# Scoring two head pairs of granule 1 ahead of their granule, with half of its queries loaded first

## The chip, the cores and the metric

The kernel runs on one core of a Trainium2 chip. The metric is the device time of one execution in microseconds (us). The engines are named as in the profile: PE (TensorE matmuls, with PEld for its weight loads), DVE (VectorE), ACT (ScalarE), POOL (GpSimd) and SP (SyncE, which here issues every DMA). The kernel before takes 595.39 us, the median of 3 runs (595.28 to 595.61).

## The reference, cut to what matters

Three layers follow one another: a windowed attention, a gated layer of 512 x 2048 x 512 with Mish, and a bilinear layer of 512 x 1536 x 512.

```python
# q, k, v: (2, 8, 768, 64)      block = 32, window = 16
k_sum = k.reshape(B, H, nb, block, D).max(axis=3)
v_sum = v.reshape(B, H, nb, block, D).mean(axis=3)
scores_l = where(|i - j| < window, scale * q @ k.T, -1e9)
scores_s = scale * einsum('bhsd,bhnd->bhsn', q, k_sum) + log(block)
a = softmax(concat([scores_l, scores_s]))          # + 1e-9 in the denominator
x = (a @ concat([v, v_sum])).transpose(0, 2, 1, 3).reshape(B * S, H * D)
h = x @ w_in;  x = (h * tanh(softplus(h))) @ w_out # Mish
return (x @ w_a) * (x @ w_b) @ w_out2
```

## The kernel before

**Attention.** The 1536 tokens form six granules of 256 tokens (g = 0 to 5; 0 to 2 are the first batch). The eight heads are four pairs p = 0 to 3; a pair fills the 128 partitions with two heads of 64. For one granule and some pairs `batch_s` (L549) multiplies queries by the 96 keys of a window and by the 24 block maxima (PE lines L567 and L571, 16 records each for a pair). `weights` (L579) then turns the scores of one pair into softmax weights: four mask-and-minimum operations on DVE (L588), four exponentials on ACT (L594), and on DVE an addition (L597), a reciprocal (L599) and the scaling (L601). `batch_o` (L606) transposes the weights (L626), copies them out of PSUM (L377 on ACT or L378 on DVE), multiplies them by the window's values (L638) and splits the result into a rounded part XH (L377 or L378) and a rest XL (L668). The weights lie in a ring of four slots, `sa_o`. Granule 0 is scored pair by pair, all others two pairs at a time.

Granule 0 doesn't wait for the block means of the values. These means are made by `prep_v` (matmuls L492), copied by `keep_v` (L503) and multiplied in at the end (L651). For later granules one DMA per granule, `spread_v` (L507, shown as `attn<-attn`), lays the means under the value windows.

**The layers behind.** A weight chunk comes raw (512 KB) into one of three stage slots and is converted by `convert` and `split`: L688 or L691 on ACT, L693 and L696 (and a further one, L700, in the unsigned form) on DVE, a rounding on ACT (L377) and a difference on DVE (L708). L688 uses the table of the exponential; the unsigned form needs no table. The first layer's chunks 0 and 1 are multiplied by granule 0 (L897 into h, Mish L927, L944 into y), then by granule 1, and so on (`visits1`, L759). The later lines, L1076, L1121 and L1229, are the rest of the two layers and fill the time from about 130 us.

**Order.** A planner (`Plan.emit`, L89) orders all instructions of an engine when the kernel is built: each operation has a key, lowered so that its users can meet theirs, and a modelled clock picks the ready operation with the lowest key on each engine. The constants at L43 to L50 are that model. A change of ACT's table adds `TABLE_PENALTY` to a key, and on PE another kind of matmul adds `SHAPE_PENALTY`. Keys below -50 are pinned; they order the first DMAs. The opening's pinned keys stand at L761, L836, L840 and L849; `bt` and `out_t` (L807 to L815) are the keys of scoring and of the output of each granule and pair. Where PE has nothing ready early on, the planner puts in idle matmuls (L434) until `fill_end` (L441). The engines then run in that order and wait on semaphores.

The first DMAs of the kernel before are, in order: keys and queries of granule 0 for the pairs 0 to 3 (384 KB and 128 KB each), the value windows of granule 0 (224, 384 and 384 KB), chunk `in` 1 of the weights, the other values of the batch (four of 256 KB), chunk `in` 0, the queries of granule 1 (512 KB), its value windows (two of 512 KB) and chunk `out` 0.

Of the kernel before, what the change touches and what calls it, by code (L numbers as in the profile page):

```python
# [34 lines left out]
class Plan:  # L35
# [8 lines left out]
    SAME, PE_SHAPE = 0.02, 0.095  # L44
    SHAPE_PENALTY = 1.6
    PINNED = -50.0
    DMA_LEAD, DMA_TAIL, DMA_RAMP = 0.62, 2.18, 8.0
    BACKLOG, DMA_SLACK, DMA_RING = 4.0, 0.5, 8
    TABLE, TABLE_PENALTY = 1.3, 5.37
    WARM, PAGE, PE_LEAD, FETCH, FETCH_BUSY = 0.34, 256, 64, (6.4, 2.6), 46.0  # L50
# [38 lines left out]
    def emit(self):  # L89
# [7 lines left out]
        key = [0.0] * n  # L97
# [10 lines left out]
        ready = {e: [] for e in engines}  # L108
        free_at = {e: 0.0 for e in engines}
        bank_free, where, held = {b: 0.0 for b in range(8)}, {}, set()  # L110
# [12 lines left out]
        while done < n:  # L123
            best = None
            for e in engines:
                t = free_at[e]
# [91 lines left out]
            if delay:  # L218
                dma_free = max(dma_free, end + self.DMA_LEAD) + delay * (1.35 if 2.0 < dma_free < self.DMA_RAMP else 1.0)
                end = dma_free + self.DMA_TAIL  # L220
                landed.append(end)
# [19 lines left out]
def attention_mish_moe_bilinear_moe(  # L241
# [90 lines left out]
    q_o = [take(NP * GT) for _ in range(NQ)]  # L332
    sa_o = [take(GU * SW) for _ in range(NSA)]
    at_o = [take(GU * P) for _ in range(NAT)]
# [7 lines left out]
    ksum_o = [take(NB) for _ in range(NP)]  # L342
    st_o = [[take(GU) for _ in range(3)] for _ in range(NSA)]
    n_ext = max(top[0] - EXT, N_EXT)
# [95 lines left out]
    pe(-1.0, 0.22 * 8, warm_up, words=16, r=["warm"], w=["warmbank"], alloc=("warmbank",), free=["warmbank"])  # L440
    pl.fill, pl.fill_end = fill, T0 + -7.99  # L441

# [97 lines left out]
    def load_q(key, g):  # L540
        b, gi = divmod(g, NG)
        o = q_o[g % NQ]

        for p0, p1 in [(p, p + 1) for p in range(NP)] if g == 0 else [(0, NP)]:
            dma(key + 1.0 * p0, ar(o, NP, GT)[:, p0:p1, :],
                qT[b, p0:p1, :, gi * GT:(gi + 1) * GT].rearrange("n d t -> d n t"),
                w=[sb(o + p0 * GT, (p1 - p0) * GT)], nbytes=(p1 - p0) * P * GT * 4)

    def batch_s(key, g, ps):  # L549

        b, gi = divmod(g, NG)
        names = [("S", g, ps, h) for h in range(2)]
        half = [slice(h * U, (h + 1) * U) for h in range(2)]
        slots = [nxt("sa", sa_o) for p in ps]
        sks = [sb(so, GU * SW) for _, so in slots]

        def mm(env):
            bk = [bank[env[name]] for name in names]
            for k, p in enumerate(ps):
                qt, kt, ks = ar(q_o[g % NQ], NP, GT)[:, p, :], ar(kt_o[p], SK), ar(ksum_o[p], NB)  # L560
                for j in range(2):
                    c = (2 * k + j) * SW

                    for h, e in ((0, 0), (1, 1), (0, 1), (1, 0)):
                        u = 2 * j + e
                        k0 = U * (GU * gi + u)
                        nc.tensor.matmul(bk[h][half[e], c:c + WK], qt[half[h], u * U:(u + 1) * U],  # L567
                                         kt[half[h], k0:k0 + WK], start=True, stop=True)
                    for h, e in ((0, 0), (1, 1), (0, 1), (1, 0)):
                        u = 2 * j + e  # L570
                        nc.tensor.matmul(bk[h][half[e], c + WK:c + SW], qt[half[h], u * U:(u + 1) * U],  # L571
                                         ks[half[h], :], start=True, stop=True)

        rd = [x for p in ps for x in (sb(q_o[g % NQ] + p * GT, GT), sb(kt_o[p], SK), ("kpad", p), sb(ksum_o[p], NB))]
        pe(key, 0.58 * len(ps), mm, words=64 * len(ps), duty=0.69, table="quarters", r=rd, w=names + sks, alloc=tuple(names))
        for k, p in enumerate(ps):
            weights(key + 0.01 * k, g, p, names, k, *slots[k], ring["sa"] - len(ps) + k, k == len(ps) - 1)

# [27 lines left out]
    def batch_o(key, g, ps):  # L606
# [7 lines left out]
        for p in ps:  # L614
            so, born = st.pop(("a", g, p))
            alive("sa", sa_o, born)
            s = ar(so, GU, SW)
# [142 lines left out]
    size = lambda b: GT * len(gran2[b])  # L760
    w_dma = {("in", 0): -88.93, ("out", 0): -85.34, ("in", 1): -93.01}  # L761
    pace = (6.36, 5.0, 6.2, 6.0, 5.4)
    att_in = {0: 4, 1: 8, 2: 8}
# [40 lines left out]

    SIGN = (T0 + 32.36, tl + 20.0)

    batches = [(g, p) for g in range(B * NG) for p in range(NP)]  # L807
    bt, out_t = {}, {}
    BG, SP = (26.14, 40, 48, 59.27, 73.73), (0.5, 1.0, 1.0, 1.08, 1.43)
    for g, p in batches:  # L810
        if g == 0:
            bt[g, p] = 5.46 + 1.76 * p
        else:
            bt[g, p] = BG[g - 1] + SP[g - 1] * p
        out_t[g, p] = bt[g, p] + (7.82 if g else 11.69)  # L815

    eps = 1.0e-3
    first_use = {}
    for vi, b, c, ts, dt in steps1:
        for kind, d in (("in", 0.0), ("out", 1.22 * dt)):  # L820
            first_use.setdefault((kind, c), ts + d)
# [10 lines left out]
    for b in range(B):  # L832
        g0 = NG * b
        if b == 0:
            pieces = [(T_S[0], 2), (T_S[2], 2)]
            kv, kd, ev = 9.86, -92.86, 1.5  # L836
        else:
            pieces = [(T_S[0], 2), (Y1, 2)]
            kv, kd = bt[g0, 0] - 3.2, bt[g0, 0] - 13.1
            ev = end_o(g0 - 2) + eps  # L840
        at_time(ev, lambda kv=kv, kd=kd, b=b, x=pieces: prep_v(kv, kd, b, x))
        at_time(ev, lambda kv=kv, b=b: keep_v(kv + 0.5, b))
        for p in range(NP):
            kk, kd = (bt[g0, p] - 4.19, -100.0 + p) if b == 0 else (bt[g0, p] - 3.0, bt[g0, 0] - 6.96 + 0.5 * p)
            ev = end_s(g0 - 1) if b else 1.0
            at_time(ev, lambda kd=kd, b=b, p=p: load_k(kd, b, p))
            at_time(ev, lambda kk=kk, p=p: prep_k(kk, p))
    for g in range(B * NG):
        kq, kw = [(-99.5, -94.0), (-85.86, -85.4)][g] if g < 2 else (bt[g, 0] - 0.92, bt[g, 0] - 4.68)  # L849
        at_time(end_s(g - 2) if g >= 2 else 1.0, lambda k=kq, g=g: load_q(k, g))  # L850
        at_time(end_o(g - 2) if g >= 2 else 1.4, lambda k=kw, g=g: load_windows(k, g))
        if g:
            at_time(end_o(g - 2) + 3 * eps if g >= 2 else 1.6, lambda k=bt[g, 0], g=g: spread_v(k, g))
    for g in range(B * NG):
        for ps in ([(p,) for p in range(NP)] if g == 0 else [(0, 1), (2, 3)]):
            at_time(bt[g, ps[0]], lambda g=g, ps=ps: batch_s(bt[g, ps[0]], g, ps))
            at_time(out_t[g, ps[0]], lambda g=g, ps=ps: batch_o(out_t[g, ps[0]], g, ps))
# [9 lines left out]
    def need(kind, c):  # L867
        if (kind, c) not in w_at:
            load_w(first_use[kind, c] - 7.48, kind, c, slot_of[kind, c])

# [34 lines left out]
    def step1(i, vi, b, c, ts, dt):  # L905
# [19 lines left out]
        gh, gl = ar(ho, n), ar(go, n)  # L925
        ka = ts + 0.3 * dt
        act(ka, n, lambda env: nc.scalar.activation(out=g, in_=hp(env), func=AF.Mish),  # L927
# [5 lines left out]
        need("out", c)  # L933
        ky = ts + 2.26 * dt
        for m in range(KC):
# [322 lines left out]

    combine_x1(A_, t - 18.9)
    combine_x1(B_, t - 1.27)  # L1260
    done_l = set()
# [81 lines left out]
```

## Time and profile before

| | |
|---|---|
| median of 3 runs | 595.39 us |
| the profiled execution | 595.54 us |
| its span in the trace | 593.8 us |
| PE busy | 586.6 us (99%) |
| PE weight loads busy | 530.9 us (89%) |
| DVE busy | 489.2 us (82%) |
| ACT busy | 318.8 us (54%) |
| DMA moved | 54.89 MB |

The span runs from the first to the last instruction on the core; 1.74 us of the execution's time lie outside it. Times of rows count from the span's start. A busy share is an average over stages that differ, and a PE that is busy can be busy with idle matmuls, or at half clock. Shares of single stretches and the granted clock are therefore read from stretches of some microseconds.

### The profile page before, as it was taken

The numbers are of one execution on the slowest core, as the hardware profiler recorded it, in microseconds if no ns is written. First come the engines' busy times: TensorE is split into PE (matmuls) and PEld (weight loads), VectorE is DVE, ScalarE is ACT, GpSimd is POOL, SyncE is SP. The second block draws the span as 40 slices with busy tenths as digits, with TensorE's granted clock in tenths as the row PEclk, the third lists the DMA queues.
The fourth block names the chain that finished last, engine by engine and source line by source line (L and its number), as shares of the span: only waits on it lengthen the run. The fifth ranks groups of instructions, "written<-read, shape, count | busy, mean of one in ns | idle before, by whom it ended". The sixth has DMA issues, their size and how long they took to land.

```text
span 593.8 us, 10770 instructions
## 1 busy us (share of the span) xinstructions
PE 586.6 (99%) x4162; PEld 530.9 (89%) x4163; DVE 489.2 (82%) x1134; ACT 318.8 (54%) x711; POOL 6.7 (1%) x34
## 2 busy tenths in 40 slices
PE   9999999999999999999999999999999999999998
PEld 5788788889898899989999999999898999999896
DVE  6899999999999988979799998858686876855443
ACT  5699999457555555455376655444262434433030
POOL 3000000000000000000000000000000000000000
PEclk9899999999999999999999999999999999999999
DMA  9997700222233221222003133230122212300202
GB/s 282 348 345 221 224 20 3 71 72 72 71 107 106 73 71 72 72 71 72 0 1 100 43 107 111 103 107 20 52 72 71 108 35 72 107 0 2 89 18 107
DMA packets 22288, 54.89 MB, mean 92 GB/s; under 512 B 1917, under 2 KB 8061, under 8 KB 22237
## 3 DMA queue, kind: packets, MB, share of 16 engines
q1 hardware_dynamic: 22236, 54.21, 27.8%
q8 instruction: 32, 0.52, 0.4%
q14 instruction: 20, 0.16, 0.1%
HBM read 50.07 MB, written 3.15 MB: 90 GB/s over the span
## 4 chain that ended last, share of the span: by engine, by line
PE 92%; ACT 3%; DVE 3%; DMA 1%; issue 1%; ACTq 0%
PE bank L1076 44%; PE bank L1121 17%; PE bank L1229 17%; PE bank L944 5%; PE bank L897 4%; ACT attn L594 2%; PE bank L567 1%; PE bank L638 1%; DMA attn<-attn 1%; PE bank L626 1%; PE bank L434 1%; DVE attn L588 1%; ACT L927 1%; ACT rounded L377 0%; PE bank L571 0%
## 5 line engine op out<-in xcount | busy, mean ns | idle before, releaser
L1076 PE MATMUL bank<-rounded,wext 128*128 128x384 f32 x1176 | 213.8, 335 | 0.0
L1076 PEld LDWEIGHTS bank<-rounded,wext 128*128 128x128 f32 x1176 | 205.7, 188 | 3.5
L377 ACT CAST rounded<-arena 128x384 fp32r<-128x384 f32 (+2 forms) x145 | 80.8, 568 | 88.9 <-PE bank L1229 37.4
L1121 PE MATMUL bank<-rounded,wext 128*128 128x512 f32 (+1 forms) x456 | 104.7, 380 | 0.0
L1229 PE MATMUL bank<-wext,rounded 128*128 128x512 f32 (+2 forms) x441 | 100.0, 386 | 0.0
L1089 DVE TENSOR_TENSOR arena<-arena,bank 128x384 f32<-128x384 f32 x132 | 71.8, 550 | 31.2 <-PE bank L1076 23.1
L1229 PEld LDWEIGHTS bank<-wext,rounded 128*128 128x128 f32 x441 | 82.0, 188 | 16.3
L1121 PEld LDWEIGHTS bank<-rounded,wext 128*128 128x128 f32 x456 | 83.9, 188 | 12.6
L1085 ACT COPY arena<-bank 128x384 f32<-128x384 f32 x108 | 51.5, 478 | 56.5 <-PE bank L1076 53.8
L377 ACT CAST wext<-arena 128x512 fp32r<-128x512 f32 (+1 forms) x80 | 49.0, 621 | 33.2 <-PE bank L1076 12.7
L1076 PE MATMUL bank<-rounded 128*128 128x384 f32 x336 | 61.1, 335 | 0.0
L1076 PEld LDWEIGHTS bank<-rounded 128*128 128x128 f32 x336 | 58.5, 188 | 0.2
L1125 DVE TENSOR_TENSOR arena<-bank,arena 128x512 f32<-128x512 f32 (+1 forms) x76 | 49.9, 658 | 10.0 <-PE bank L1121 9.9
L1248 DVE TENSOR_TENSOR arena<-bank,arena 128x512 f32<-128x512 f32 (+2 forms) x37 | 25.0, 677 | 34.5 <-PE bank L1229 34.5
L708 DVE TENSOR_TENSOR wext<-arena,wext 128x512 fp32r<-128x512 f32 (+1 forms) x80 | 49.8, 639 | 0.7 <-ACT wext L377 0.3
L696 DVE SCALAR_TENSOR_TENSOR arena<-arena 128x512 uint32<-128x512 uint32 x68 | 46.6, 689 | 2.3 <-ACT arena L688 0.4
L708 DVE TENSOR_TENSOR rounded<-arena,rounded 128x384 fp32r<-128x384 f32 (+2 forms) x72 | 40.9, 583 | 4.8 <-ACT rounded L377 4.3
L594 ACT ACTIVATE attn<-attn 128x120 f32<-128x120 f32 x96 | 36.7, 386 | 7.6 <-DVE attn L588 7.5
L944 PE MATMUL bank<-rounded 128*128 128x512 f32 (+1 forms) x168 | 37.1, 367 | 0.0
L688 ACT ACTIVATE arena<-arena 128x512 f32<-128x512 f32 x38 | 25.8, 680 | 17.7 <-DMA arena<-in_w_out_dram 9.4
L897 PE MATMUL bank<-rounded 128*128 128x512 f32 (+1 forms) x168 | 35.3, 363 | 0.0
L897 PEld LDWEIGHTS bank<-rounded 128*128 128x128 f32 x168 | 28.1, 189 | 4.7
(75 smaller groups left out, 546.3 us busy)
## 6 DMA issues: line engine op xcount, KB each, us to landing
arena<-in_w_out_dram SPq DMA_DIRECT2D x28, 512.0 KB, 3.3
arena<-in_w_in_dram SPq DMA_DIRECT2D x16, 512.0 KB, 3.9
arena<-in_w_a_dram SPq DMA_DIRECT2D x12, 512.0 KB, 4.1
arena<-in_w_b_dram SPq DMA_DIRECT2D x12, 512.0 KB, 3.3
arena<-in_kT_dram SPq DMA_DIRECT2D x8, 384.0 KB, 9.6
out_dram<-arena SPq DMA_DIRECT2D x11, 256.0 KB, 2.0
attn<-in_qT_dram SPq DMA_DIRECT2D x5, 512.0 KB, 8.7
attn<-in_v_dram SPq DMA_DIRECT2D x3, 768.0 KB, 7.3
```

The source lines that it names most:

```text
L377: alts = [("ACT", act_us(n), lambda env: nc.scalar.copy(out=dst(env), in_=src(env))), ("DVE", dve2_us(n) if fast else dve_us(n), lambda en ...
L594: act(key, SW + 90, lambda env, x=x: nc.scalar.activation(out=s[:, x, :], in_=s[:, x, :], func=AF.Exp, scale=-1.0, bias=negm[:, x:x + 1], ...
L696: dve(key, 512, lambda env: nc.vector.scalar_tensor_tensor(out=f.bitcast(U32), in0=hw.bitcast(U32), scalar=3, in1=f.bitcast(U32), op0=ALU. ...
L708: dve(key, n, lambda env: nc.vector.tensor_sub(out=r32(lo[0]()), in0=src, in1=hi[0]()), r=rd + hi[1], w=lo[1])
L897: nc.tensor.matmul(like(dst, b), lt, rt, start=(j == 0), stop=(j == 3 * KC - 1))
L944: nc.tensor.matmul(yp, lt, r32(rt), start=(fst and j == 0), stop=(lst and j == 2))
L1076: nc.tensor.matmul(dst, lt, r32(rt), start=(start and i == 0 and j == 0), stop=(last and i == 1 and j == 2), skip_group_check=True)
L1085: act(k, TN, lambda env: nc.scalar.copy(out=dst[0], in_=bank[env[nm[z]]][:, 0:TN]), w=[nm[z]] + dst[1])
L1089: dve(k, TN, lambda env: op(out=dst[0], in0=dst[0], in1=bank[env[nm[z]]][:, 0:TN]), w=dst[1] + [nm[z]], free=[nm[z]] if free else [])
L1121: nc.tensor.matmul(dst, lt, rt, start=(q == 0), stop=(q == 5))
L1125: dve(k + 1.2, n, lambda env: nc.vector.tensor_add(acc, bank[env[yn]][:, 0:n].rearrange(*shape[2], **shape[3]), acc), w=[yn] + ak, free=[yn])
L1229: nc.tensor.matmul(dst, lt, rt, start=(opens and j == 0), stop=(closes and j == n_mm - 1))
```

## The change

Granule 1's queries come in two DMAs of 256 KB. The first one, for the pairs 0 and 1, has the key -97.2, between the queries of pair 2 and the keys of pair 3 of granule 0; the second keeps a place behind the value windows. The pairs 0 and 1 of granule 1 are scored singly (keys 8.0 and 20.0), and their weights lie in two further slots that use the memory of `T_S[2]`. Their output has the key 15.97 + 7.59. The values of the first batch come in two DMAs of 512 KB into `Y0`, ahead of both `in` chunks, and their means are one block of matmuls and no longer two. The pinned keys, several planner constants and many keys of the rest are set anew. The diff, cut to its core:

```diff
-    SHAPE_PENALTY = 1.6
+    SHAPE_PENALTY = 1.69
-    DMA_LEAD, DMA_TAIL, DMA_RAMP = 0.62, 2.18, 8.0
+    DMA_LEAD, DMA_TAIL, DMA_RAMP = 0.62, 1.62, 8.0
+    START, RAMP = 0.8, ((2.8, 1.0), (7.3, 1.75), (11.0, 1.0), (1.0e9, 0.95))
-    TABLE, TABLE_PENALTY = 1.3, 5.37
+    TABLE, TABLE_PENALTY = 1.3, 11.05
...
-    sa_o = [take(GU * SW) for _ in range(NSA)]
+    sa_o = [take(GU * SW) for _ in range(NSA)] + [T_S[2], T_S[2] + GU * SW]
...
-    pl.fill, pl.fill_end = fill, T0 + -7.99
+    pl.fill, pl.fill_end = fill, T0 + -11.04
...
-        for p0, p1 in [(p, p + 1) for p in range(NP)] if g == 0 else [(0, NP)]:
-            dma(key + 1.0 * p0, ar(o, NP, GT)[:, p0:p1, :],
+        for p0, p1 in [(p, p + 1) for p in range(NP)] if g == 0 else ([(0, 2), (2, NP)] if g == 1 else [(0, NP)]):
+            dma(-97.2 if g == 1 and p0 == 0 else key + 1.0 * p0, ar(o, NP, GT)[:, p0:p1, :],
...
-        slots = [nxt("sa", sa_o) for p in ps]
+        first = g == 1 and ps[0] < 2
+        slots = [(NSA + p, sa_o[NSA + p]) if first else nxt("sa", sa_o[:NSA]) for p in ps]
...
-    w_dma = {("in", 0): -88.93, ("out", 0): -85.34, ("in", 1): -93.01}
-    pace = (6.36, 5.0, 6.2, 6.0, 5.4)
+    w_dma = {("in", 0): -89.93, ("out", 0): -86.62, ("in", 1): -91.35}
+    pace = (6.36, 4.44, 6.2, 6.0, 5.4)
...
-    SIGN = (T0 + 32.36, tl + 20.0)
+    SIGN = (T0 + 28.01, tl + 20.0)
...
-    BG, SP = (26.14, 40, 48, 59.27, 73.73), (0.5, 1.0, 1.0, 1.08, 1.43)
+    BG, SP = (26.14, 40.37, 50.16, 59.27, 72.77), (0.5, 1.0, 1.0, 0.61, 1.43)
...
-            bt[g, p] = 5.46 + 1.76 * p
+            bt[g, p] = 5.74 + 1.76 * p
...
-        out_t[g, p] = bt[g, p] + (7.82 if g else 11.69)
+        if g == 1 and p < 2:
+            bt[g, p] = (8.0, 20.0)[p]
+        out_t[g, p] = (15.97 if g == 1 and p < 2 else bt[g, p]) + (7.59 if g else 11.69)
...
-            pieces = [(T_S[0], 2), (T_S[2], 2)]
-            kv, kd, ev = 9.86, -92.86, 1.5
+            pieces = [(Y0, 4)]
+            kv, kd, ev = 7.92, -92.3, 1.5
...
-        kq, kw = [(-99.5, -94.0), (-85.86, -85.4)][g] if g < 2 else (bt[g, 0] - 0.92, bt[g, 0] - 4.68)
+        kq, kw = [(-99.5, -94.0), (-86.84, -85.05)][g] if g < 2 else (bt[g, 0] - -0.41, bt[g, 0] - 4.28)
...
-        for ps in ([(p,) for p in range(NP)] if g == 0 else [(0, 1), (2, 3)]):
-            at_time(bt[g, ps[0]], lambda g=g, ps=ps: batch_s(bt[g, ps[0]], g, ps))
+        for ps in ([(p,) for p in range(NP)] if g == 0 else [(0,), (1,), (2, 3)] if g == 1 else [(0, 1), (2, 3)]):
+            at_time(bt[g, ps[0]], lambda g=g, ps=ps: batch_s(bt[g, ps[0]], g, ps))
...
-            load_w(first_use[kind, c] - 7.48, kind, c, slot_of[kind, c])
+            load_w(first_use[kind, c] - 8.99, kind, c, slot_of[kind, c])
...
-    combine_x1(A_, t - 18.9)
-    combine_x1(B_, t - 1.27)
+    combine_x1(A_, t - 18.29)
+    combine_x1(B_, t - 0.29)
```

The times of the visits, `t`, are sums of `pace`, so every key that hangs on `t` behind granule 1's two chunks is 2 x 0.56 us lower.

## Rows read from the trace of the kernel before

**Rows 1.** The page: busy us of the engines, share of the span, instructions.
```profile
PE 586.6 (99%) x4162; PEld 530.9 (89%) x4163; DVE 489.2 (82%) x1134; ACT 318.8 (54%) x711; POOL 6.7 (1%) x34
```
**Rows 2.** Waits of PE behind 20 us: place, releaser, us in total, times, longest.
```profile
PE bank L626 <- DVE attn L601: 1.6, 3, 0.6
PE bank L638 <- DMA attn<-attn: 0.5, 1, 0.5
PE bank L626 <- ACT arena L927: 0.4, 1, 0.4
```
**Rows 3.** Stretches: length, busy us of PE, PEld, DVE, ACT, POOL; clock, DMA share, GB/s.
```profile
10.00:15.00 5.00, 5.00 (x119) 3.64 (x113) 4.97 (x27) 4.57 (x22) 0.00 (x0) 1.00 1.08 347
15.00:20.00 5.00, 4.54 (x90) 3.33 (x88) 3.84 (x10) 2.41 (x6) 0.08 (x1) 1.00 1.09 367
20.00:25.00 5.00, 5.00 (x122) 4.09 (x126) 4.49 (x18) 2.99 (x9) 0.43 (x1) 0.75 1.07 364
25.00:30.00 5.00, 4.58 (x61) 4.32 (x54) 4.89 (x31) 5.00 (x24) 0.00 (x0) 0.91 1.07 305
...
80.00:100.00 20.00, 20.00 (x298) 16.72 (x297) 19.46 (x73) 18.89 (x60) 0.00 (x0) 1.00 0.01 2
```
**Rows 4.** Short stretches, columns as before: where the clock falls and rises.
```profile
22.50:22.75 0.25, 0.25 (x10) 0.25 (x12) 0.25 (x2) 0.25 (x2) 0.00 (x0) 0.53 1.19 434
...
26.00:26.50 0.50, 0.50 (x5) 0.50 (x6) 0.50 (x6) 0.50 (x5) 0.00 (x0) 1.00 0.98 381
```
**Rows 5.** PE's timeline: start, us, line, operands, count; idle before it and releaser.
```profile
5.79 1.68 PE L434 MATMUL bank<-attn 128*128 128x512 bf16 x7
...
11.15 0.81 PE L434 MATMUL bank<-attn 128*128 128x512 bf16 x3
...
21.75 0.40 PE L567 MATMUL bank<-arena,attn 64*64 64x96 f32 x8
...
22.33 0.61 PE L567 MATMUL bank<-arena,attn 64*64 64x96 f32 x5
...
25.84 3.17 PE L897 MATMUL bank<-rounded 128*128 128x256 f32 x24
...
29.86 0.62 PE L626 MATMUL bank<-attn 128*120 128x128 f32 x4 [0.42 <-DVE attn L601]
...
33.32 0.62 PE L626 MATMUL bank<-attn 128*120 128x128 f32 x4 [0.50 <-DVE attn L601]
34.59 0.62 PE L626 MATMUL bank<-attn 128*120 128x128 f32 x4 [0.65 <-DVE attn L601]
```
**Rows 6.** The chain that ended last: start, us until the next step, what.
```profile
12.14 0.57 DVE attn L601
12.71 1.22 DVE attn L588 x12
...
14.61 0.09 DVE attn L599
...
15.53 0.33 DVE arena L693
...
15.96 0.71 DVE arena L696
...
58.44 5.95 DMA attn<-attn
```
**Rows 7.** DVE's timeline, columns as for PE.
```profile
16.57 0.65 DVE L601 TENSOR_TENSOR attn<-attn 128x480 f32<-128x480 f32 x1
...
23.50 0.75 DVE L668 TENSOR_TENSOR rounded<-bank,rounded 128x256 fp32r<-128x256 f32 x2
```
**Rows 8.** ACT's timeline, columns as for PE.
```profile
15.24 0.66 ACT L688 ACTIVATE arena<-arena 128x512 f32<-128x512 f32 x1
...
31.88 1.28 ACT L927 ACT_TABLE_LOAD   x1
33.17 0.66 ACT L927 ACTIVATE arena<-bank 128x256 f32<-128x256 f32 x2
```

More of the change, by code (lines that the diff above doesn't have):

```diff
@@ L108, in emit @@
         ready = {e: [] for e in engines}
-        free_at = {e: 0.0 for e in engines}
+        free_at = {e: self.START for e in engines}
         bank_free, where, held = {b: 0.0 for b in range(8)}, {}, set()
@@ L218, in emit @@
             if delay:
-                dma_free = max(dma_free, end + self.DMA_LEAD) + delay * (1.35 if 2.0 < dma_free < self.DMA_RAMP else 1.0)
+                dma_free = max(dma_free, end + self.DMA_LEAD) + delay * next(f for lim, f in self.RAMP if dma_free < lim)
                 end = dma_free + self.DMA_TAIL
@@ L342, in attention_mish_moe_bilinear_moe @@
     ksum_o = [take(NB) for _ in range(NP)]
-    st_o = [[take(GU) for _ in range(3)] for _ in range(NSA)]
+    st_all = take(3 * GU * (NSA + 2))
+    st_o = [[st_all + GU * (3 * i + j) for j in range(3)] for i in range(NSA + 2)]
     n_ext = max(top[0] - EXT, N_EXT)
@@ L576, in batch_s @@
         for k, p in enumerate(ps):
-            weights(key + 0.01 * k, g, p, names, k, *slots[k], ring["sa"] - len(ps) + k, k == len(ps) - 1)
+            weights(key + 0.01 * k, g, p, names, k, *slots[k], None if first else ring["sa"] - len(ps) + k, k == len(ps) - 1)
     def weights(key, g, p, names, k, i, so, born, last):
@@ L615, in batch_o @@
             so, born = st.pop(("a", g, p))
-            alive("sa", sa_o, born)
+            if born is not None:
+                alive("sa", sa_o[:NSA], born)
             s = ar(so, GU, SW)
@@ L819, in attention_mish_moe_bilinear_moe @@
     for vi, b, c, ts, dt in steps1:
-        for kind, d in (("in", 0.0), ("out", 1.22 * dt)):
+        for kind, d in (("in", 0.0), ("out", 1.34 * dt)):
             first_use.setdefault((kind, c), ts + d)
@@ L834, in attention_mish_moe_bilinear_moe @@
         if b == 0:
-            pieces = [(T_S[0], 2), (T_S[2], 2)]
-            kv, kd, ev = 9.86, -92.86, 1.5
+            pieces = [(Y0, 4)]
+            kv, kd, ev = 7.92, -92.3, 1.5
         else:
             pieces = [(T_S[0], 2), (Y1, 2)]
-            kv, kd = bt[g0, 0] - 3.2, bt[g0, 0] - 13.1
+            kv, kd = bt[g0, 0] - 6.04, bt[g0, 0] - 9.78
             ev = end_o(g0 - 2) + eps
@@ L843, in attention_mish_moe_bilinear_moe @@
         for p in range(NP):
-            kk, kd = (bt[g0, p] - 4.19, -100.0 + p) if b == 0 else (bt[g0, p] - 3.0, bt[g0, 0] - 6.96 + 0.5 * p)
+            kk, kd = (bt[g0, p] - 4.14, -100.0 + p) if b == 0 else (bt[g0, p] - 3.0, bt[g0, 0] - 7.58 + 0.5 * p)
             ev = end_s(g0 - 1) if b else 1.0
@@ L925, in step1 @@
         gh, gl = ar(ho, n), ar(go, n)
-        ka = ts + 0.3 * dt
+        ka = ts + 0.44 * dt
         act(ka, n, lambda env: nc.scalar.activation(out=g, in_=hp(env), func=AF.Mish),
@@ L933, in step1 @@
         need("out", c)
-        ky = ts + 2.26 * dt
+        ky = ts + 2.4 * dt
         for m in range(KC):
```

## The prediction

> **What bounds the kernel now.** I read the page first, then the waits of PE, then PE's timeline of the opening and at last DVE's, ACT's and the chain. The page has PE at 99% of the span [rows 1], so the time is what PE has to do plus what it loses, and it loses nearly all of it early: from 80 us on a stretch shows 20.00 busy us of 20, at full clock [rows 3], while the waits behind 20 us sum to 1.6 + 0.5 + 0.4 = 2.5 us [rows 2]. Nothing behind the opening can give more than that. In the opening itself PE's busy share misleads twice. First, it holds 17 idle matmuls (L434, from 5.79 to 11.96; first and last group in [rows 5]). Second, the granted clock stands at half from 22.5 to about 25.9 us [rows 4], and PE did four pairs' scoring of granule 1 there: the first pair took 22.33 - 21.75 = 0.58 us at full clock, the other three 25.84 - 22.33 = 3.51 us, 1.17 each [rows 5]. At full clock they would be 1.74, so 1.77 us are lost to the clock.
>
> Then comes L897, the first layer, at 25.84. Its operand was ready earlier: the last XL of granule 0 ends at 23.50 + 0.75 = 24.25 [rows 7]. So 1.6 us of L897's start are PE's own queue. Behind it PE waits three times for the scaled weights of granule 1 (L626 behind L601: 0.42, 0.50, 0.65, together 1.57 us) [rows 5]. DVE is the engine behind those waits: it is busy 4.97, 3.84, 4.49 and 4.89 us of 5 in the four stretches from 10 to 30 us [rows 3]. Its idle time from 10 to 25 us is 0.03 + 1.16 + 0.51 = 1.70 us. ACT in the same time is idle 0.43 + 2.59 + 2.01 = 5.03 us and then full, 5.00 of 5.
>
> **Part 1: queries earlier.** 256 KB (0.262 MB) go in front of the keys of pair 3. At 347 to 367 GB/s, with the DMA engines at 1.07 to 1.09 of their time [rows 3], all that follows lands 0.7 to 0.75 us later, except what is moved. SP issues one more DMA. Pair 3 of granule 0 is scored 0.7 us later; I charge nothing, since DVE, which is full then, ends that pair's L601 only at 16.57 + 0.65 = 17.22 [rows 7]. Uncovered it would be the 0.75. PE takes the early pair's matmuls in order: if its queries were late, granule 0's pair 2 would stand behind them on PE, and DVE behind that. The same 0.75 bounds it.
>
> **Part 2: the values ahead of the weights.** The values of the batch no longer stand behind chunk `in` 1 (512 KB) but behind the 256 KB of queries: 0.7 us earlier. The means are now one block, which starts only when all is there, so I take 0.3 us gain for L651, with 0 and 0.7 as its ends. Chunk `in` 1 lands behind 1280 KB more (256 of queries, 1024 of values), 1.31 MB by 0.36 = 3.6 us later; before, it was on ACT at 15.24 [rows 8], so now about 18.9. Its conversion leaves the full stretch before 17 us (L693 and L696, 0.33 + 0.71 = 1.04 us of DVE [rows 6]) and comes to lie beside that of chunk `in` 0, which lands 0.7 later. Both and XL compete for DVE from 19 to 24.5 us.
>
> **Part 3: two pairs ahead.** A pair costs PE 0.58 us [rows 5] and DVE, by the steps of the chain, 4 x 1.22/6 for L588, 0.09 each for L597 and L599 and 0.57 for L601 [rows 6]: 1.56 us. Pair 0 lies among the idle matmuls: on PE it is free. On DVE it has a lower key than granule 0's pairs 2 and 3 and goes ahead of them: +1.56 - 1.04 (the conversion gone) = 0.5 us later for the last pair of granule 0, of which the 0.3 of part 2 hides nothing, because it is another input of L651 and XL. The second pair (key 20.0) falls into 18.4 to 22 us, where DVE has its idle 1.2 us, or behind XL. So XL ends between 24.0 and 25.2 us; I take 24.7, half a microsecond after 24.25. L897 then starts at 24.7, 1.1 us before 25.84, with the pairs 2 and 3 (2 x 0.58 = 1.16 us) still to be scored behind it. **Balance at this point: 0.** Its ends: -1.8, if all of the half-clock loss goes; +2.5, if the half clock falls on L897 (rival C).
>
> **Part 4: what follows L897.** The exponentials of the pairs 0 and 1 are done by then, and so are L601 and much of the transposing. Before, Mish had to wait behind 16 exponentials: L897 ended at 25.84 + 3.17 = 29.0, Mish came at 33.17, behind a table load of 1.28 us [rows 5, 8]. Now ACT has no exponentials ready when h is, so Mish goes first and L944 gives PE work while the pairs 2 and 3 go through DVE and ACT. The three waits of 1.57 us lose their cause. What limits the gain is DVE's ledger: work pulled ahead of 25 us must fit into 1.70 us of idle DVE. Both limits agree on 1.6; I take **-1.4**, with 0 and -1.6 as ends. What is late next: the output of granule 1 also needs `spread_v`, whose DMA took 5.95 us for granule 3 [rows 6]. It is issued behind the value windows, which land 0.7 us later, and no earlier than before.
>
> **Part 5: the rest.** The waits at 54 and 65 us (0.4 for Mish, 0.5 for a spread [rows 2]) have keys that move by a microsecond or less: 0, ends -0.9 and +0.9. The earlier `SIGN` bound turns those weight chunks whose keys lie between T0 + 28.0 and T0 + 32.4 to the unsigned form; one more DVE operation like L696, 0.71 us [rows 6], perhaps twice. By then PE has work queued: 0, at most +1.4. A higher `TABLE_PENALTY` saves loads of 1.28 us on ACT [rows 8], which costs PE little (0.4 in rows 2): 0, at best -0.4. Two slots more, single-pair banks and fewer idle matmuls: 0, for nothing waits for them; a lack of banks would show as PE waits of the size in [rows 2], 0.5.
>
> **Sum**: 0 - 1.4 = -1.4 us. The profiled execution took 595.54 us (span 593.8 and 1.74 around it), 0.15 above the median of 595.39; from the median the sum gives **594.0 us**.
>
> **Rivals.** A is the forecast: 594.0, by itself 593.2 to 594.8.
>
> B: the waits come back in another form. Pairs 2 and 3 are scored no earlier (about 27.7 to 28.9 us against 25.84 at the latest before), so their L601 is as late as before, and if granule 1's output is held by the spread, PE has L944 to do but then waits. For it: DVE is as full behind 25 us as before [rows 3]. Against it: half of that work is gone. Gain 0.2 to 0.6: 595.0.
>
> C: slower, by the clock. Between L651 and L897 PE now has one pair to score where it had four. Before, the clock fell at 22.5 us, behind the small matmuls of L651, and came back at 25.9 behind dense scoring [rows 4, 5]. With PE waiting from 22 to 24.7 it may fall again and stay low under L897, whose 24 matmuls take 3.17 us at full clock [rows 5]: half of them at half clock cost 1.6, all 3.2 us. With 0.4 left of part 4's gain the price is +1.2 to +2.8: 597.4. It decides once L897 runs at 1.2 GHz for more than half of its matmuls. The Trainium skill has this as a rule ("TensorE: Matmul & The Clock Gate", section "HAM oscillation — how this bites in real kernels"): matmuls that stop to wait for data come back at the cold clock, and the cost is paid anew behind each such wait. By that rule the change goes wrong here, and the trace agrees in part: PE lost 1.77 us in this place with hardly a wait. I give it 0.14 because the pair that is scored at about 20 to 22 us puts dense work where L651 stood alone.
>
> D: more than forecast. V, XL and both conversions are in time, L897 starts near 24.2 at full clock, so 1.2 of the 1.77 us come back on top of part 4, and the wait for the spread goes too: -2.6 to -3.4, 592.5.
>
> E: the change doesn't do what it says: pair 1 ends up behind L897 and pair 0 alone is early. Then PE saves 0.58 in the idle matmuls and part of the waits: -0.6, 594.8.
>
> **How the numbers follow.** A 0.40, B 0.20, C 0.14, D 0.18, E 0.08. A measurement of this kernel can tell about 0.2% (1.2 us) from no change, so "faster" is below 594.2. Of A some 0.28 lie below it and 0.12 above; with D and a little of E and B faster is 0.50. Same: 0.12 of A, nearly all of B and E, some of C's lower end: 0.36. Slower: C, 0.14. The range that leaves out 2 in 10 cuts D below 592.2 and C above 596.6.
>
> **What would show it.** Right: a pair of L567 between 8 and 11 us and one near 20; L897 starting at 24 to 25 us; Mish and L944 before the exponentials of pairs 2 and 3; no waits of L626 for L601 between 28 and 35 us. Wrong: a clock of 0.5 under L897; L601 of granule 0's pair 3 later than 18 us; XL later than 25.2; new waits of PE for DMA or L668 before 40 us; or waits between 45 and 70 us that sum to well over 0.9.

## The result, and the profile after

The changed kernel takes **601.03 us** (median of 4 runs, 600.75 to 601.45); the kernel before, run beside it, 595.5 (595.28 to 596.36). The ratio is 1.009, interval 1.0075 to 1.0105: slower by 5.5 us, where 594.0 was predicted and 596.6 was the upper end. The profiled execution took 601.45 us with a span of 599.5.

The page after, line for line beside [rows 1]: PE is less busy by 1.5 us, in a span that is 5.7 us longer. So the loss is not added work: PE stood, or ran slowly.

```profile
PE 585.1 (98%) x4148; PEld 530.1 (88%) x4148; DVE 485.7 (81%) x1122; ACT 321.6 (54%) x721; POOL 6.8 (1%) x34
```

To find the place I take the starts of the first layer's groups of matmuls (L904 after is L897 before; lines shift by 2 to 7). Both kernels reach them with the same work behind them, idle matmuls apart; only in front of the first L904 the changed kernel has eight transposes of granule 1 more (L630 at 24.94). The second visit ends where the first group of 512 columns starts:

| us | first L904 | second visit | first 512-column group | second one | third one | end of span |
|---|---|---|---|---|---|---|
| before | 25.84 | 39.73 | 43.32 | 58.43 | 72.53 | 593.84 |
| after | 27.79 | 40.06 | 43.65 | 64.39 | 78.90 | 599.51 |
| difference | +1.95 | +0.33 | +0.33 | +5.96 | +6.37 | +5.67 |

The opening loses 1.95 and gets 1.62 back; 1.0 us of both is the transposes, which changed their place. One stretch, from 43.65 to 64.39, takes 20.74 us where it took 15.11: this is the loss, +5.63, and the rest of the kernel moves along.

PE's waits in the profile after, from 5 us on (place, releaser, us in total, times, longest), answer to [rows 2]:

```profile
PE bank L494 <- issue: 4.3, 2, 3.0
PE bank L574 <- DVE attn L464: 1.7, 2, 1.1
PE bank L494 <- DVE attn L600: 1.4, 1, 1.4
PE bank L570 <- DMA attn<-in_qT_dram: 1.4, 2, 0.8
PE bank L642 <- DMA attn<-attn: 1.0, 1, 1.0
```

The three waits for the scaled weights are gone, as forecast. What stands first is "issue", 4.3 us in two times: PE waits for nothing that the profile shows. PE's timeline of the profile after has both, and most of the loss:

```profile
16.66 0.85 PE L494 MATMUL bank<-attn 80*24 80x128 f32 x23 [1.29 <-issue]
...
27.79 3.13 PE L904 MATMUL bank<-rounded 128*128 128x256 f32 x24
...
48.82 1.27 PE L494 MATMUL bank<-attn 80*24 80x128 f32 x32 [1.39 <-DVE attn L600]
...
51.28 1.15 PE L642 MATMUL bank<-attn 120*64 120x64 f32 x32
...
55.47 0.64 PE L494 MATMUL bank<-arena,attn 128*24 128x128 f32 x16 [3.04 <-issue]
56.03 2.93 PE L951 MATMUL bank<-rounded 128*128 128x256 f32 x12
```

PE waits 1.39 us at 48.82 and stands 3.04 us at 55.47, together 4.43, where the kernel before has one wait of 0.39 in this stretch (L626 at 54.14, the 0.4 in [rows 2]). And PE's busy time in it is 16.32 us, where it was 14.72: 1.60 more, of which 1.24 are the twelve matmuls L951, which took 2.93 us here and 1.69 in a run at full clock (below). 4.43 - 0.39 + 1.60 is the 5.63, but for rounding. The stretches of the profile after show the slow matmuls in the clock (columns as in [rows 3]):

```profile
52.43:55.43 3.00, 0.00 (x0) 0.00 (x0) 3.00 (x11) 2.54 (x8) 0.00 (x0) 1.00 0.35 127
55.50:59.50 4.00, 4.00 (x33) 3.79 (x33) 0.53 (x6) 3.27 (x5) 0.00 (x0) 0.57 0.44 135
59.50:64.40 4.90, 4.90 (x131) 4.46 (x129) 3.79 (x8) 0.80 (x3) 0.00 (x0) 1.00 0.01 3
```

In the first one DVE is full, but the chain of the profile after (start, us, what) doesn't lead PE's stand back to it; it leads the wait at 48.82 back to a weight chunk that was 8.28 us on its way:

```profile
39.31 8.28 DMA arena<-in_w_in_dram
...
48.64 0.09 DVE attn L600
48.73 0.09 issue
48.82 1.27 PE bank L494 x32
...
51.35 1.08 PE bank L642 x32
52.43 3.04 issue
55.47 0.64 PE bank L494 x16
```

The first of the sixteen L494 at 55.47 has no semaphore to wait for in the trace. What it waited for can be read from the page's list of DMA queues:

```profile
q1 hardware_dynamic: 22220, 54.21, 27.2%
q8 instruction: 32, 0.52, 0.4%
```

0.52 MB in 32 packets is 16 KB each, and PE has 2 x 4148 matmuls and weight loads: a packet for each 256 or so. So I read these packets as PE's instructions. PE's stands fit that step. They come at the 440th and the 1710th of PE's records (matmuls and weight loads, counted in order of time), which are 1270 = 5 x 254 apart. I call such a place a border: there PE comes to the first instruction of a new packet. In the profile after, a packet of this queue ran at 40.57 and the next one only at 52.98, for 1.07 us; PE went on 1.4 us behind its end. The DMA answers for those two stretches of the profile after (48.0 to 52.9, then 52.9 to 54.1):

```profile
q1 hardware_dynamic: 865, 1.73, 101.0%
```

```profile
q1 hardware_dynamic: 84, 0.18, 39.5%
q8 instruction: 1, 0.02, 5.6%
```

The packet that PE needs at the 1710th record runs some time after PE crossed the border before it, the 1456th. In the profile after, PE crossed that one at 49.02 and was through with its 254 records at 52.43, in 3.41 us; the packet ran 3.96 us behind the crossing, when the data queue ran dry. In the kernel before, PE crossed its own 1456th record at 44.71, the packet ran at 47.72, and PE needed it only at 51.30, 6.59 us behind the crossing: no stand. So two things set the stand, how quickly PE uses up 254 records and how long the packet takes to come.

The load of a weight chunk that is in the queue ahead of this packet comes with the change. SyncE's timelines, before and after, show the next two loads of `in` chunks; the first one was issued behind the packet that ran at 52.00, and now goes out at 48.67, ahead of the one that runs at 52.98:

```profile
52.12 1.54 SPq L364 DMA_DIRECT2D arena<-in_w_in_dram  x2
48.67 6.71 SPq L366 DMA_DIRECT2D arena<-in_w_in_dram  x2
```

### The profile page after: what moved, and what is told of

Read it like the earlier page. It is cut to its first block, busy times and chain, and to the rows that moved or that the text cites. A ratio compares the mean times of both kernels' runs of the same rounds, so it can differ in the third digit from the quotient of the medians.

```text
span 599.5 us, 10697 instructions
## 1 busy us (share of the span) xinstructions
PE 585.1 (98%) x4148; PEld 530.1 (88%) x4148; DVE 485.7 (81%) x1122; ACT 321.6 (54%) x721; POOL 6.8 (1%) x34
## 3 DMA queue, kind: packets, MB, share of 16 engines
q1 hardware_dynamic: 22220, 54.21, 27.2%
## 4 chain that ended last, share of the span: by engine, by line
PE 90%; DMA 4%; DVE 3%; ACT 2%; issue 1%; SPq 0%
PE bank L1083 44%; PE bank L1128 17%; PE bank L1236 16%; PE bank L951 5%; PE bank L904 4%; DMA arena<-in_w_out_dram 1%; DMA arena<-in_w_in_dram 1%; PE bank L630 1%; PE bank L642 1%; ACT attn L597 1%; PE bank L494 1%; DMA arena<-in_kT_dram 1%; PE bank L570 1%; DVE attn L464 0%; DVE arena L700 0%
## 5 line engine op out<-in xcount | busy, mean ns | idle before, releaser
L379 ACT CAST rounded<-arena 128x384 fp32r<-128x384 f32 (+3 forms) x151 | 83.2, 565 | 85.5 <-PE bank L1236 37.8
L712 DVE TENSOR_TENSOR rounded<-arena,rounded 128x384 fp32r<-128x384 f32 (+1 forms) x72 | 40.3, 583 | 3.9 <-ACT rounded L379 3.5
L951 PE MATMUL bank<-rounded 128*128 128x512 f32 (+1 forms) x168 | 39.6, 380 | 0.1
L597 ACT ACTIVATE attn<-attn 128x120 f32<-128x120 f32 x88 | 33.7, 387 | 8.9 <-DVE attn L591 8.7
L692 ACT ACTIVATE arena<-arena 128x512 f32<-128x512 f32 x38 | 26.0, 684 | 20.4 <-DMA arena<-in_w_out_dram 12.9
L904 PE MATMUL bank<-rounded 128*128 128x512 f32 (+1 forms) x168 | 35.1, 362 | 0.0
L951 PEld LDWEIGHTS bank<-rounded 128*128 128x128 f32 x168 | 29.2, 198 | 5.3 <-DVE rounded L672 0.4
```

Source lines behind the costliest of these rows:

```text
L379: alts = [("ACT", act_us(n), lambda env: nc.scalar.copy(out=dst(env), in_=src(env))), ("DVE", dve2_us(n) if fast else dve_us(n), lambda en ...
L597: act(key, SW + 90, lambda env, x=x: nc.scalar.activation(out=s[:, x, :], in_=s[:, x, :], func=AF.Exp, scale=-1.0, bias=negm[:, x:x + 1], ...
L712: dve(key, n, lambda env: nc.vector.tensor_sub(out=r32(lo[0]()), in0=src, in1=hi[0]()), r=rd + hi[1], w=lo[1])
L904: nc.tensor.matmul(like(dst, b), lt, rt, start=(j == 0), stop=(j == 3 * KC - 1))
L951: nc.tensor.matmul(yp, lt, r32(rt), start=(fst and j == 0), stop=(lst and j == 2))
```

## The experiments

The theory after the result: PE's instructions come in packets over the same DMA engines as the data, and the change made PE cross one such border, with quick matmuls behind it, while a queue of weights and keys was ahead of the packet. The first rival: the early pairs themselves cost the time on DVE and ACT. The second: the stand belongs to this place in the program. The runs came in three batches, each with the kernel before beside it: 596.03, 595.78 and 595.80 us. The changed kernel wasn't run again, so a time in a batch is compared with its 601.03 by the ratios to the kernel before (the changed kernel's is 1.009). Every timeline is that of one execution.

**Moving the borders.** Tiny matmuls in the warm-up shift all later instructions against the borders; the planner's order stays.

```diff
-        for _ in range(8):
+        for _ in range(6):
             fill(env["warmbank"])
+        for _ in range(26):
+            nc.tensor.matmul(bank[env["warmbank"]][0:32, 0:32], warm[:, 0:32], warm[:, 0:32], start=True, stop=True)
```

> The changed kernel with the same order on every engine; only the opening's 8 idle matmuls of 512 columns become 6 of them and 26 of 32 columns, so that PE's instruction stream has 48 words more ahead of everything else. Theory (code loading): in the trace of the changed kernel PE stands still from 52.43 to 55.47 us ahead of an L494 that has no semaphore to wait for, and a 16 KB packet of the instruction queue moves at 52.98 to 54.05; the same happens 256 x 5 records earlier, at 15.4 to 16.66. With 48 words more that border falls on about 43 us instead of 48.8, PE is still in the slow L904 then, and the code is there in time: the wait of 3.04 us and the half clock behind it (L951 x12 in 2.93 us instead of 1.6) go, 601.0 - 3.0 - 1.5 = 596.5 us (596.0 to 597.5). Rival (data: that L494 waits for the values' DMA or for a bank that ACT or DVE holds): nothing changes, 600.5 to 601.5.

Measured: 598.59 us, ratio 1.0047 (1.0031 to 1.0063), 2.4 less than the changed kernel, but over the 597.5 that was the end of the expected range. Its timeline at the place:

```profile
51.77 1.15 PE L644 MATMUL bank<-attn 120*64 120x64 f32 x32
52.85 0.64 PE L496 MATMUL bank<-arena,attn 128*24 128x128 f32 x16
53.42 1.69 PE L953 MATMUL bank<-rounded 128*128 128x256 f32 x12
```

The same matmuls follow without a stand and at full clock; the stretch takes 15.71 us. Here is also the 1.69 used above. The opening lost 1.9 us more: it has a stand of 1.59 at 16.02 and half clock from 15.97 to 22.80, where the changed kernel has 1.29 at 16.66 and half clock from 18.48 to 21.89.

> As the run with 48 words, with 96 more (6 idle matmuls of 512 columns and 50 of 32). Theory (code loading): the borders fall on about 40 and 51 us; the page that begins at 51 is loaded while DMA traffic falls off, so the wait is at most 1 us: 596 to 598 us. Rival (data): 600.5 to 601.5.

Measured with 50 tiny matmuls: 598.71 us, 1.0049 (1.0027 to 1.0071), over a wide spread of 596.81 to 603.57; 596 to 598 was expected. The stretch took 16.21 us in the profiled one (597.89), without the stand. By both runs the stand isn't part of this place in the program.

**The kernel before, shifted by 192 instructions** (5 warm-up matmuls and 99 tiny ones).

> The kernel before with the same order on every engine and 192 words more in front (5 idle matmuls of 512 columns and 99 of 32), so that a border between two pages of instructions falls on the dense small matmuls at about 49 us, as it does in the changed kernel. Theory (code loading): PE, which has no early pairs here, gets the same wait of 2 to 4 us between 52 and 56 us with half clock behind it: 598 to 601 us. Rivals (data, or the early pairs themselves): 595.5 us, up to 0.7 more for the longer idle matmuls.

Measured: 597.05 us, 1.0017 (1.0007 to 1.0026). A miss: I had wanted the same stand at 52 us. PE crossed a border at 50.65 and was through with its 254 records at 54.13, in 3.48 us, as quickly as in the changed kernel. But the packet ran at 51.53, 0.88 behind the crossing, in a DMA queue that was near its end (share 0.94 from 51.50 to 52.50, 0.28 from 52.50 to 54.00), and the stretch took 15.04. The profiled execution is 1.7 us later than the kernel before at the end of the stretch, and all of that comes from the opening, from a stand of 1.11 and a longer half clock. So quick matmuls behind a border make no stand by themselves; the queue has to be there too.

**The shift told to the planner** (50 tiny matmuls, its lead for borders 160 for 64, and its span of slow packets 58 us for 46).

> The changed kernel planned anew with 96 words more in front (as in the run with 96) and with the planner told of them and of the slow loading of code up to 58 us of its time instead of 46. Theory (code loading is the loss, the early pairs by themselves gain nothing): about the kernel before, 594.5 to 597 us. Rival (the early pairs cost by themselves what the kernel lost): 599 to 601 us. Rival (they gain what was forecast and only the loading hid it): below 594.3 us.

Measured: 601.78 us, 1.0101 (1.0072 to 1.0131). A miss too: the planner made another opening, with the first layer at 32.04. Its stretch behind that took 15.34 us, without a stand, but with so much else moved nothing follows from the total.

**The shift put in at 33 us**, 24 tiny matmuls ahead of the first L642 of granule 1, so that the opening stays.

```diff
+            if e == "PE":
+                if pe_ops == 30:
+                    self.words(next(b for b in bank_free if b not in held and bank_free[b] <= t), 24)
+                pe_ops += 1
```

> The changed kernel with the same order on every engine and 24 idle matmuls of 32 columns (48 words) put in ahead of the first L642 of granule 1, where PE waits 0.96 us for a DMA anyway. The opening stays as it is, and only the borders behind 33 us move. Theory (code loading costs 4.5 to 5 us between 44 and 64 us, as the runs with 48 and 96 words in front showed while they lost 0.5 to 2 us in the opening): the time from the first L904 of 512 columns to the second falls from 20.7 to 15.5 to 16.5 us, and the whole to 595.7 to 597. Rival (the gain of those two runs came from something their opening did): 600.5 to 601.5.

Measured: 598.01 us, 1.0047 (1.003 to 1.0064), from 597.15 to 603.47; neither 595.7 to 597 nor the rival's 600.5 to 601.5. The profiled execution is the 603.47, the longest of all:

```profile
56.02 1.55 PE L652 MATMUL bank<-attn 120*64 120x64 f32 x24 [3.60 <-issue]
```

The stand is there again, at the same 1710th record, but now under L652 (L642 after), another instruction. And the packet was due earlier: PE came to the 1456th record at 44.02, 5.0 us before it did after (49.02). It ran at 53.57 all the same, 9.55 us later. The DMA answers for 44.0 to 53.5 and for 53.5 to 54.7:

```profile
q1 hardware_dynamic: 1290, 2.77, 104.5%
```

```profile
q1 hardware_dynamic: 138, 0.28, 64.2%
q8 instruction: 1, 0.02, 5.6%
```

So the place in the program doesn't set the stand. Nor does PE's pace here: PE crossed earlier than in the changed kernel, and the packet came no sooner, but when the data queue ended. Most other executions of this kernel are some 5 us faster; that they escape the stand fits, but wasn't seen, since only this one has a trace.

**Less data in the queue.** Four loads of raw weight chunks (issued at 39.31, 42.76, 48.67 and 55.05 us in the changed kernel, so three of them ahead of the packet) move 64 KB and not 512 KB; the order of all engines stays. What isn't loaded is computed with old weights.

```diff
-        dma(kd, ar(so, 1024).bitcast(U32), w_dram[kind][c].bitcast(U32), w=[sb(so, 1024)], nbytes=P * 4096)
+        def load(env):
+            raws.append(c)
+            n = 128 if 7 <= len(raws) <= 10 else 1024
+            nc.sync.dma_start(out=ar(so, 1024)[:, 0:n].bitcast(U32), in_=w_dram[kind][c].bitcast(U32)[:, 0:n])
+
+        pl.add(kd, [("SP", 0.48, load)], w=[sb(so, 1024)], delay=P * 4096 / 3.3e5)
```

> The changed kernel with the 7th to the 10th load of a raw weight chunk (the ones issued at 39.31, 42.76 and two from 48.67 us) cut to 128 of 1024 columns, 64 KB in place of 512 KB; the rest of these chunks is left as it was, so the layers are computed with old weights there. The order of all engines stays. Theory (the loaded DMA engines delay PE's instruction packet): about 1.8 MB less, some 5 us of transfer, so the packet that began at 52.98 begins within 1 us of its crossing, the stand of 3.04 us falls below 0.8, the half clock at 56.0 to 59.4 goes, and the wait of 1.39 for the chunk issued at 39.31 goes too; the stretch from the visit-2 end at 43.65 to the first 512-column group takes 15.0 to 16.0 us against 20.74, and the median is 595.2 to 596.8. Rival (PE uses up a page of instructions in 3.6 us and no packet could come in time, whatever the DMA load): the stand stays at 2 to 3 us, the median at 598.5 to 600. Rival (a wait in the program that the trace doesn't show): the stand of 3.04 stays.

> The kernel before with the same cut of its 7th to 10th weight load (old weights for the rest of these chunks). It says what the cut gives by itself. In the kernel before the packet came 0.5 us behind the crossing at 51.5, so all theories expect next to nothing: 594.9 to 595.6 (part of the waits of 0.4 and 0.5 us may go). The difference between the two cut kernels, by the theory 0 to 1.8 us, is then what the change costs without its late packet; if the cut kernel before gained 3 us or more, the DMA load would be a cost of its own in both.

Measured: the changed kernel 597.49 us, 1.0027 (1.0017 to 1.0038); the kernel before with the same cut 595.96, 1.0003 (0.9995 to 1.0012). So the cut is worth nothing in the kernel before and 3.5 us in the changed one (0.6% by the ratios). The thinned changed kernel at the place, and its DMA share (last column but one) in two stretches:

```profile
47.80 1.08 PE L494 MATMUL bank<-attn 80*24 80x128 f32 x32 [0.39 <-DVE arena L704]
...
52.42 0.64 PE L494 MATMUL bank<-arena,attn 128*24 128x128 f32 x16 [1.22 <-issue]
52.99 1.69 PE L958 MATMUL bank<-rounded 128*128 128x256 f32 x12
```

```profile
48.00:50.00 2.00, 2.00 (x96) 1.79 (x88) 1.82 (x9) 1.99 (x6) 0.00 (x0) 1.00 0.98 316
50.00:52.00 2.00, 1.21 (x44) 1.03 (x35) 2.00 (x8) 1.97 (x4) 0.00 (x0) 1.00 0.19 57
```

The queue ends at 50 and not at 53, and the packet runs at 49.95 and not at 52.98. The stand falls from 3.04 to 1.22, not below 0.8 as expected; the wait from 1.39 to 0.39; the half clock goes. The stretch takes 16.20 us: 4.54 of the 5.63 are back. The median is 0.7 above the theory's range; the stand of 1.22 that is left fits that. PE was through with its 254 records in 3.4 us here too, so even this packet, 2.15 us behind its crossing, came too late.

**One part at a time.** The kernel before with the early pairs alone (half load, single scoring, two slots; the values go to `Y0` and `Y1`, since the slots take their memory); the changed kernel without them; and the changed kernel with pair 0's weights keyed 9 us later:

```diff
-            weights(key + 0.01 * k, g, p, names, k, *slots[k], ...)
+            weights(key + (9.0 if first and ps[0] == 0 else 0.0) + 0.01 * k, g, p, names, k, *slots[k], ...)
```

> The kernel before with the early half of granule 1's queries and the early scoring of its pairs 0 and 1 alone (two more slots; the values go to Y0 and Y1, still in four DMAs); all other keys and constants as before. Read by stages, since the borders of the code pages fall anew behind the opening. Theory (the weights of both pairs go ahead of granule 0's on DVE and ACT, and code loading is at its limit in the opening): L897 starts 1.5 to 3.5 us later than 25.84, and the second visit (L897 of granule 1) starts at 39.5 to 41. Rival (it is the new order of the values and weights that delays L897): L897 starts at 25 to 26.3.

> The changed kernel without the early queries and the early scoring (granule 1's queries in one DMA, its pairs two at a time, keys from BG); all else as changed. Theory (early pairs delay the opening): L904 starts at 25.3 to 26.5 us, but the second visit then no earlier than 39.5. Rival (the rest of the new order delays it): L904 starts behind 27 us. The total hangs on where the borders of the code pages fall: 594.5 to 600.

> The changed kernel with pair 0 of granule 1 scored as early, but its softmax weights given a key that is 9 us later, behind those of granule 0's pairs. Theory (these weights on DVE and ACT delay granule 0): granule 0's last L604 ends by 17.5 us instead of 18.57 and L904 starts at 26 to 27.2 instead of 27.79. Rival (the wait for code at 15.4 to 16.66 us and the half clock behind it set L904): no earlier than 27.5.

Measured: 598.98 (1.0054, 1.0041 to 1.0067), 602.71 (1.0139, 1.0104 to 1.0173) and 606.64 us (1.0179, 1.0166 to 1.0192). With the pairs alone the first layer starts at 29.30, behind a stand of 1.73 that ends at 16.09. Without them it starts at 25.34, with half of its matmuls (the others follow at 28.21), but then come a wait of 1.57, a stand of 1.92 at 39.34 and half clock from 40.1 to 43.5, and the second visit is at 43.71. Later weights put the first layer at 32.57, behind a stand of 2.69. By the start of the first layer the first two came as the theory of early pairs said (27.3 to 29.3, and 25.3 to 26.5), the third against it (26 to 27.2). But each has its stand in another place: every edit of the plan moves the borders, so these three don't tell the parts' own cost apart.

**Do the early pairs cost the opening?** Their weights are made on 16 of 120 columns; PE's and SP's order stay.

```diff
+        W = 16 if g == 1 and p < 2 else SW
...
-                out=s[:, x, :], in0=bank[env[names[h]]][:, c:c + SW], in1=mask[:, var, :],
+                out=s[:, x, 0:W], in0=bank[env[names[h]]][:, c:c + W], in1=mask[:, var, 0:W],
```

> The changed kernel in which the score weights of the early pairs 0 and 1 of granule 1 are made on 16 of 120 columns (DVE's masks, ACT's exponentials, the scaling); the other columns are zero, so these two pairs are computed wrongly. Order of PE and SP as before it; two small instructions of DVE trade places. Theory 1 (in the opening DVE and ACT pay for the pairs ahead of granule 0, 1.56 us of DVE each): granule 0's last scaling starts at 16.8 or earlier against 17.91, L904 starts at 25.5 to 26.5 against 27.79, and the median is 599.0 to 600 if the stand at 55 us stays. Theory 2 (it is the instruction packets and the order of the loads): the scaling moves by less than 0.5, L904 still starts at 27.3 or later, and the median stays within 0.7 us of 601.0.

Measured: 601.70 us, 1.0097 (1.0075 to 1.0119), from 598.55 to 603.77; L906 (L904) at 28.58 and a stand of 3.04 at 56.21. PE's timeline:

```profile
17.42 0.85 PE L495 MATMUL bank<-attn 80*24 80x128 f32 x23 [1.08 <-issue]
20.55 1.96 PE L632 MATMUL bank<-attn 128*120 128x128 f32 x8
...
28.58 3.14 PE L906 MATMUL bank<-rounded 128*128 128x256 f32 x24
```

This speaks against theory 1: less work on DVE gave nothing (granule 0's last scaling came at 18.49, after a later start of the whole opening, which wasn't explained). From the packet's stand on to the first layer PE takes 28.58 - 17.42 = 11.16 us, and 27.79 - 16.66 = 11.13 in the changed kernel, without a wait in either. So behind that stand neither DVE nor ACT holds PE up; what they cost in front of it, this run doesn't show. The cut was a weak one on ACT, though, where an exponential still took 0.29 us each and not 0.38.

**One constant back:** weight chunks asked for 7.48 us ahead of use and not 8.99.

```diff
-            load_w(first_use[kind, c] - 8.99, kind, c, slot_of[kind, c])
+            load_w(first_use[kind, c] - 7.48, kind, c, slot_of[kind, c])
```

> The changed kernel with one constant set back: later weight chunks are asked for 7.48 and not 8.99 us ahead of their first use. Its opening is the same up to about 30 us. Theory (loaded DMA at the crossing): if the two loads issued from 48.67 us now come behind the packet, the stand of 3.04 shrinks to under 1.5 and the median is 596.5 to 599; if the planner leaves them in front of it, the time stays at 600 to 601.5. Rival (the stand belongs to PE's pace, not to the loads): 600 to 601.5 wherever they are.

Measured: 601.42 us, 1.0088 (1.0074 to 1.0103), from 599.70 to 602.46; the profiled execution is the 599.70. The first of the two `in` loads now goes out at 51.21, the packet ran ahead of it at 50.83, 0.62 behind its crossing, the stand of 3.04 is gone and the stretch takes 15.32 us. But at 37.80 PE had a wait that it didn't have in the changed kernel, and half clock from 39.0 to 42.5 with it:

```profile
37.80 0.62 PE L630 MATMUL bank<-attn 128*120 128x128 f32 x4 [2.26 <-DVE attn L604]
```

Expected was 596.5 to 599 if the stand went. In this execution it went, and the gain went into another pause; what the executions at 601.4 us lose was not seen. No run here beats the kernel before; by the two thinned kernels the change is 1.5 us slower even with most of its late packet away.

## Why the prediction was wrong, point by point

**Bound and place.** PE is the bound, and the opening is where time is lost: right. That nothing behind the opening can *give* much was right as well; that nothing behind it can *cost* much doesn't follow, and I let it stand.

**Parts 1 and 2: the loads.** Chunk `in` 1 was forecast on ACT at 18.9; L692 started at 18.80. For later queries I charged nothing; PE then had waits for queries and block maxima (1.4 and 1.7 us in the list above). All of these fall before 14 us, where [rows 5] has idle matmuls, and what they cost behind that was not separated.

**Part 3: the balance of 0 at the first layer.** This step failed first. L897 was to start at 24.7 and started at 27.79, 1.95 us later than before. The eight transposes of granule 1 that stand in front of it now stood behind it before, and they are 1.0 us of this (Part 4 has the number); the step's own loss is the other 0.9 us. The rows show where it came from. Pair 0 went ahead of granule 0's pairs 2 and 3, as forecast, but the masks of pair 1 went ahead of pair 3's scaling on DVE too, at 16.64 to 17.7 and not from 18.4 on; that scaling started at 17.91 against 16.57 [rows 7], 1.34 us later and not 0.5. PE stood 1.29 us for a packet at 16.66. And the half clock didn't go away: it came from 18.48 to 21.89, where eight transposes took 1.96 us; at full clock, at 24.94, eight took 1.09. The step looked for the operand that comes last. It should have summed PE's queue: from 16.66 PE doesn't wait once. The last XL comes at 27.11, behind PE's own work (PE's and then DVE's timeline of the profile after):

```profile
19.57 1.96 PE L630 MATMUL bank<-attn 128*120 128x128 f32 x8
24.94 1.09 PE L630 MATMUL bank<-attn,arena 128*120 128x128 f32 x8
...
17.91 0.66 DVE L604 TENSOR_TENSOR attn<-attn 128x480 f32<-128x480 f32 x1
...
27.11 0.42 DVE L672 TENSOR_TENSOR rounded<-bank,rounded 128x256 fp32r<-128x256 f32 x1
```

How the 0.9 divides among these wasn't separated; e11 speaks against DVE behind 16.66.

**Part 4: -1.4.** The number came, but mostly by luck. From the first to the second visit PE took 13.89 us before and 12.27 after, -1.62. Of this, PE's busy time is 12.32 before and 11.31 after, -1.01: that is the transposes, which PE did in front of the first layer, so they are no gain. The waits are 1.57 before and 0.96 after: -0.61 is what the step gained. The three waits for scaled weights went, as forecast, and one of 0.96 for the spread at 33.14 came, the one named as "what is late next". Mish did not go first: the eight exponentials of the pairs 2 and 3 stood in front of it on ACT, and it came at 32.83, where it had come at 33.17 [rows 8]:

```profile
31.53 1.28 ACT L934 ACT_TABLE_LOAD   x1
32.83 0.66 ACT L934 ACTIVATE arena<-bank 128x256 f32<-128x256 f32 x2
```

Parts 3 and 4 together were to give 1.4 us and cost 0.33.

**Part 5: the rest, 0 with ends of 0.9.** This step failed by most: it held +5.63. It priced the waits behind 45 us by their keys, which move by a microsecond. It left out a transfer that has no key, PE's own instructions, and it said nothing of the longer lead of the weight chunks (8.99 for 7.48), which the diff has. The stand for the packet is 3.04 us of the loss, and half clock behind it most of another 1.60; with the lead set back (e12) that stand is gone. The wait of 1.39 at 48.82 is the same queue seen from the data's side, a chunk that took 8.28 us.

**The rivals.** C had the sign and not the place: L904 ran at full clock. Half clock came from 18.48 to 21.89, in front of it, and under L951 from 56.03 to 59.44. The rule that the prediction took from the Trainium skill ("TensorE: Matmul & The Clock Gate", section "HAM oscillation — how this bites in real kernels"), that matmuls come back cold from a wait for data, agrees with the trace only in part. Behind the stand of 3.04 us the clock is 0.57 of full in the row from 55.50 to 59.50, behind the stand of 1.29 at 16.66 it falls to half at 18.48, and behind e12's wait of 2.26 it is low from 39.0 to 42.5. But the waits of 0.96 at 33.14 and 1.39 at 48.82 left it at full, as did those of 0.42 to 0.65 before [rows 5], and in the kernel before it fell at 22.5 us with hardly a wait in front [rows 3, 4].

**The signs.** Of my signs for wrong all came but the first, half clock under L897. Granule 0's last scaling ended at 18.57, behind 18. The last XL came at 27.11, behind 25.2. A new wait for a DMA came at 33.14. And the waits between 45 and 70 us sum to 4.43, well over 0.9. Of my signs for right, the waits of L626 for L601 are gone and pair 0 was scored early; but pair 1 was scored before 14 us and not near 20, the first layer was late, and Mish came behind the exponentials.

## What to carry to other kernels

Read the instruction queue's row too: the code of this long unrolled kernel is a transfer that nothing in the program asks for, and it came late when data was queued. Before an edit that reorders PE or the loads, find where PE crosses from one packet to the next, how quickly it uses up the instructions behind that border, and what is queued on the DMA engines then. Where PE is the bound, forecast the start of a stage by the sum of PE's queue in front of it, not by its last operand. And before a gain between two marks is counted, look whether work has only moved across one of them.

## What the runs showed of the hardware

- A packet of 16 KB of PE's instructions ran some time behind PE's crossing of the border 254 records ahead of its use: 0.70 us with the data queue running dry (before: 51.30 to 52.00), 2.15 in the thinned kernel (47.80 to 49.95), 3.96 after (49.02 to 52.98), and 9.55 in e5 (44.02 to 53.57). Each of these four took 1.07 to 1.29 us, and where PE stood for it, its first instruction ran some 1.4 us behind the packet's end. From the crossing to that instruction it was 6.45 us in the changed kernel, and PE had used up its 254 records in 3.41; the difference is the stand of 3.04.
- The same plan can differ much from run to run: e2 spread over 6.8 us and e5 over 6.3, where the kernel before spread over 2. That some executions meet the packet in time and others don't would explain it; it is not shown, since each run has one trace.
- An exponential on 16 columns took ACT 0.29 us, on 120 columns 0.38: with an eighth of the columns three quarters of the time were left.
